# Fourier transform and gated feed-forward layer on one core: moving setup work off VectorE, one gather ahead of a bulk load, half-width copies, and a new order of the last output pieces

## The chip, the core and the metric

The kernel runs on one core of a Trainium2 chip. The metric is device time in microseconds (us) of that core; the time before is 616.64 us, the median of three runs (616.6 to 617.27). The span in a trace is some 1.9 us shorter than the time of the same run, so I compare times with times and spans with spans.

## The reference

```python
def _attn_ref(x):                       # x: (8, 3008, 256), float32
    X = np.fft.fft(x, axis=1)           # along the sequence
    X = np.fft.fft(X, axis=2)           # along the width
    return X.real.astype(np.float32)

def _moe_ref(x, w_gate, w_val, w_out):  # x: (24064, 256); 256 -> 1536 -> 256
    g = x @ w_gate
    gelu = 0.5 * g * (1.0 + erf(g * inv_sqrt2))
    val = x @ w_val
    return (gelu * val @ w_out).astype(np.float32)
# reference: _moe_ref(_attn_ref(x).reshape(24064, 256), ...)
```

## The kernel before

The sequence transform of 3008 points is done as two transforms of 32 and 94 points. x is folded first (row i plus its mirror image), so x is read twice: forward rows by a plain DMA and mirrored rows by an indirect gather. For the first batch both go through GpSimd's queue with a cast to bf16, in this order:

```python
def opening():
    ...                                  # stage[0]: forward rows 9-16 and 0, by another queue
    pool_consts()
    index_consts(0)
    cast_mirror(0, 9, 8)                 # gather, rows 9..16
    pool_consts2()
    cast_mirror(0, 5, 4)                 # gather, rows 5..8
    cast_forward(0, 1, 8)                # plain, rows 1..8
    index_consts(1)
    cast_mirror(0, 0, 1)                 # gather, row 0
    cast_mirror(0, 1, 4)                 # gather, rows 1..4
    ...                                  # weights, then x of the second batch, same queue
```

VectorE folds the rows into `eo_sb`. TensorE transforms them (`s1`), ScalarE copies the result to `A_sb`; column transforms (`ch`) give four pieces of `Z_sb`, and `tp_e` gives E and O, the two halves of the transformed x that the gate and value products read. `warm(n)` multiplies zeros n times to keep TensorE's clock up. The opening of the program is one straight list of such calls:

```python
    fold_piece(9, 4)
    first, second = fold_ops(0, 13, 4, nc.vector)
    first(); t_reduced(); second()
    s1(0, 2, 0)(); s1(0, 2, 1)()
    t_sin(); gelu_table(); warm(6)
    fold_piece(5, 4)
    s1(0, 1, 0)(); s1(0, 1, 1)()
    fold_piece(0, 1)
    fold_piece(1, 4)
    ...
```

The last chunk of tokens is written in eight pieces, (sub, half) from (3,0) to (2,1). Each is a product of twelve matmuls into a PSUM buffer (PSUM is the memory that TensorE writes), a copy to an SBUF buffer, and a store. There are three such SBUF buffers, and a buffer is free only when its store has landed:

```python
def osb_tile():
    return work([128, 2, C], FP32, "osb", 3, "out_sb")

            if last(ci):
                osb = osb_tile()
                if sign == 0:
                    nc.vector.tensor_copy(osb[:m, 0, :], pso[:m, half])
                    store(b, ci, sub, 0, osb[:, 0, :], nc.sync)
                else:
                    nc.scalar.activation(osb[:m, 1, :], pso[:m, half], AF.Copy)
                    store(b, ci, sub, 1, osb[:, 1, :], nc.scalar)
```

Of the kernel before, what the change touches and what calls it, by code (L numbers as in the profile page):

```python
# [9 lines left out]
FP32 = mybir.dt.float32  # L10
BF16 = mybir.dt.bfloat16
AF = mybir.ActivationFunctionType
# [16 lines left out]
def kernel(  # L29
# [225 lines left out]
    rd = work([128, 2 * NGP + NK], FP32, "Z", 1, "rd")  # L255
    cf, cr, cd = (work([128, C], FP32, t, 4, f"small_{i}") for i, t in enumerate(("v", "v", "v")))
    tf, tr, td = (work([128, 128], FP32, t, 3, f"small_t{i}") for i, t in enumerate(("ve", "ve", "ve")))
    w_raw = work([128, 2, 2, F], BF16, "h", 2, "w_raw")
# [69 lines left out]
    def g_phases():  # L328
# [14 lines left out]
        c = _sub(rd, [[1, NGP]], 0, part_num=NP)  # L343
        nc.vector.scalar_tensor_tensor(c, d1, -1.0, d1, op0=ALU.mult, op1=ALU.max)
        nc.vector.tensor_scalar(c, c, -0.25, None, op0=ALU.add)
        nc.vector.scalar_tensor_tensor(d0, r[:, 0:NK], MAGIC, f[:, 0:NK], op0=ALU.subtract, op1=ALU.subtract)

# [40 lines left out]
    def identities():  # L388

        nc.vector.tensor_scalar(  # L390
            _sub(II, [[128, 3], [1, 128]], 0), _sub(row_c, [[0, 3], [1, 128]], 0), col_p, None, op0=ALU.is_equal)
        nc.vector.tensor_scalar(II[:, 1, 1, :], row_c, col_p, -1.0, op0=ALU.is_equal, op1=ALU.mult)

# [196 lines left out]

    def tp_e(b, gi, g=0, engine="A", tag=None):
        def run():
            st = state(b)
            if b not in EO_bufs:
                EO_bufs[b] = EO_tiles()
            ps = psum(tag) if tag else ps_any(b)
            for pair, o, n in pairs(gi):
                nc.tensor.matmul(  # L598
                    ps[:, o : o + n], st["Z"][:, pair, g * 128 : g * 128 + 128], _sub(TP, [[1, n]], g * 128),
                    start=True, stop=True)  # L600
            if b == 0 and g == 1:
                for pair, o, n in pairs(gi):
                    nc.tensor.matmul(  # L603
                        ps[0:1, o : o + n], st["Z"][:, pair, 128:129], _sub(TP, [[1, n]], 0), start=True, stop=True)
            n = chunk_len[gi]
            dst = _sub(EO_bufs[b][g], [[1, n]], chunk_off[gi])
            if engine == "A":
                nc.scalar.activation(dst, ps[:, :n], AF.Copy)  # L608
            else:
                nc.vector.tensor_copy(dst, ps[:, :n])  # L610
        return run
# [65 lines left out]
    def ffn_work(b):  # L677
# [126 lines left out]
        for ci in range(NG):  # L804
            nsub = (chunk_len[ci] + 127) // 128
            parts = {k: [f(ci, fc) for fc in range(NFC)] for k, f in (
                ("G", l1_gate), ("V", l1_value), ("g", l1_gate2), ("v", l1_value2))}
            subs = [nsub - 1, *range(nsub - 1)] if last(ci) else range(nsub)
            l2s = [l2_piece(ci, s, g, f) for s in subs for g in range(2) for f in range(0, NFC, L2P)]
            chunks.append((parts, l2s))  # L810
# [3 lines left out]
    def opening():  # L814
# [10 lines left out]
        cast_mirror(0, 5, 4)  # L825
        cast_forward(0, 1, 8)
        index_consts(1)
        cast_mirror(0, 0, 1)
        cast_mirror(0, 1, 4)
        for f0, n in ((0, 256), (256, 256), (512, 512), (1024, 512)):  # L830
# [23 lines left out]
        vec_fills()  # L854
        warm(16)
        cw_phases()
        g_phases()
        columns = t_columns()
        g_rows(9, 7)
        cw_reduced()  # L860
        vec_fills2()
        vec_consts2()
        identities()
        cw_magnitude()
        cw_sin()
        cw_rest()
        g_ends()
        g_rows(1, 8)
        t_phases(columns)
        fold_piece(9, 4)  # L870
        first, second = fold_ops(0, 13, 4, nc.vector)
        first()
        t_reduced()
        second()
        s1(0, 2, 0)()
        s1(0, 2, 1)()
        t_sin()
        gelu_table()
        warm(6)
        fold_piece(5, 4)  # L880
        s1(0, 1, 0)()
        s1(0, 1, 1)()
        fold_piece(0, 1)
        fold_piece(1, 4)
        s1(0, 3, 0)()
        s1(0, 3, 1, "V")()
        warm(1)
        s1(0, 0, 0)()
        s1(0, 0, 1, "V")()
        minus, copies = [], []  # L890
        make_w(0, 0, 256, m_at=minus, tag="o", copy_at=copies)()
        t_write()
        for pp in range(2):
            ch(0, pp, qs=(0,))()
            ch(0, pp, "V", qs=(1,))()
        copies.pop()()
        make_w(1, 0, 256, m_at=minus, m_engine="V", tag="v", copy_at=copies)()
        tp_e(0, 0, 0, "A", tag="v")()
        tp_e(0, 0, 1, "V", tag="dft")()
        copies.pop()()  # L900
        minus[0]()
# [4 lines left out]
    def plan():  # L906
# [10 lines left out]
        for s, f in (  # L917
                (0, make_w(0, 256, 256, m_engine="P")), (0, make_w(1, 256, 256, engine="V", m_engine="P")),
                (1, make_w(1, 512, 512, (1,), m_engine="P")), (1, lambda: load_wo(0)), (1, lambda: load_wo(1)),
                (2, make_w(0, 512, 512, (0,), "V")), (2, make_w(0, 512, 512, (1,))),  # L920
                (3, make_w(1, 512, 512, (0,))), (4, make_w(1, 1024, 512, (1,), "V")),
# [146 lines left out]
```

## Time and profile before

| what | before |
|---|---|
| span of the profiled run, us | 614.93 |
| TensorE busy | 605.4 us, 98% |
| first fold starts / last fold ends | 8.26 / 13.41 |
| last of ScalarE's and VectorE's copies to `A_sb` ends | 14.89 |
| last of the four copies to `Z_sb` ends | 16.35 |
| O complete | 17.91 |
| first gelu starts | 18.37 |
| last output copy starts | 610.95 |

From the first gelu on TensorE is full, so the table is read from the top: each row is a point that the next one waits for.

Three lines of the timeline of the kernel before (start, length, engine, line, operation, tiles, count) are the issue of the forward rows 1 to 8, the tiny column products that prepare the last transform, and the first fold of rows 5 to 8.

```profile
4.85 0.60 POOL L185 DMA_DIRECT2D xb<-in_x_dram  x1
...
7.57 1.27 PE L397 MATMUL ps_v<-one,par 1*128 1x1 f32 x10
...
11.35 0.19 DVE L221 TENSOR_TENSOR eo_sb<-xb 94x8 bf16<-94x8 bf16 x1
```

The transfer's landing records (16 rings, one for each DMA engine) run from 10.21 to 11.16 us, and VectorE folds the rows at 11.35.

At the end, in the same view, the last product and the last copy:

```profile
609.44 1.47 PE L778 MATMUL ps_g<-Wo_sb,h_sb 128*128 128x256 bf16 x12
...
610.95 0.38 ACT L794 ACTIVATE out_sb<-ps_g 128x256 f32<-128x256 f32 x1 [2.24 <-DMA out_dram<-out_sb]
```

The product ends at 609.44 + 1.47 = 610.91, and the copy starts 0.04 us later. So the copy waits for TensorE, although the bracket puts its 2.24 us of idle time down to a store, the releaser that came last by the profile's account.

### The profile page before, as it was taken

What the parts mean: (1) busy time and instruction counts of PE and PEld (TensorE: products, weight loads), DVE (VectorE), ACT (ScalarE), POOL (GpSimd) and SP (SyncE); (2) the same over time, 40 slices, a digit from 0 to 9 for tenths busy, and PEclk for the clock granted to TensorE, in tenths of its full rate; (3) what the DMA queues carried; (4) which work ended last, traced back from release to release, by engine and by line L of the source; (5) the groups of instructions that cost most, each with busy time, mean ns of one, the idle gap of its engine ahead of it and who ended that gap; (6) DMA issues with size and microseconds to landing.
All of it is one profiled execution on the core that took longest, in us unless ns stands there. A gap on an engine that the chain in (4) does not pass through costs nothing.

```text
span 614.9 us, 12747 instructions
## 1 busy us (share of the span) xinstructions
PE 605.4 (98%) x4181; PEld 406.9 (66%) x4229; DVE 577.3 (94%) x941; ACT 425.0 (69%) x824; POOL 508.9 (83%) x513
## 2 busy tenths in 40 slices
PE   8999999999999999999999999999999999999997
PEld 4466666666666666666666666666666666666666
DVE  8799999999999999999999999999999999999992
ACT  6888677777776777667766677666776676666661
POOL 8999899999987999789997899869997655565551
PEclk8999999999999999999999999999999999999999
DMA  9962834547253364532553344533213223111123
GB/s 175 200 137 57 237 95 117 141 116 189 80 144 92 100 163 119 140 100 58 157 150 94 106 107 107 146 102 100 64 49 77 62 87 78 42 46 47 37 51 83
DMA packets 52466, 65.40 MB, mean 106 GB/s; under 512 B 7629, under 2 KB 47278, under 8 KB 50004
## 3 DMA queue, kind: packets, MB, share of 16 engines
q1 hardware_dynamic: 45472, 49.03, 30.5%
q0 software_dynamic: 6608, 15.29, 11.7%
q8 instruction: 33, 0.54, 0.4%
q10 hardware_dynamic: 320, 0.26, 0.2%
q14 instruction: 33, 0.27, 0.2%
HBM read 39.65 MB, written 30.17 MB: 114 GB/s over the span
## 4 chain that ended last, share of the span: by engine, by line
PE 94%; DVE 2%; issue 1%; DMA 1%; ACT 1%; SPq 1%; POOL 0%; DVEq 0%; POOLq 0%; ACTq 0%
PE ps_o L778 39%; PE ps_g L681 29%; PE ps_v L681 20%; PE ps_dft L562 2%; PE ps_dft L598 2%; DMA out_dram<-out_sb 1%; PE ps_dft L451 1%; SPq L675 1%; PE ps_o L847 0%; PE ps_dft L542 0%; ACT gelu_sb L705 0%; ACT gelu_sb L714 0%; DVE v_sb L751 0%; POOL h_sb L753 0%; PE ps_dft L603 0%
## 5 line engine op out<-in xcount | busy, mean ns | idle before, releaser
L753 POOL TENSOR_TENSOR h_sb<-gelu_sb,v_sb 128x512 bf16<-128x512 bf16 (+1 forms) x280 | 319.9, 1147 | 87.0 <-DVE v_sb L751 79.0
L778 PE MATMUL ps_o<-Wo_sb,h_sb 128*128 128x256 bf16 (+1 forms) x2232 | 334.3, 272 | 0.0
L778 PEld LDWEIGHTS <-h_sb 128*128 128x128 bf16 (+1 forms) x2304 | 228.6, 100 | 111.2 <-POOL h_sb L753 1.0
L733 DVE SCALAR_TENSOR_TENSOR ve_sb<-EB_sb,yw,ps_v 128x512 f32<-128x512 bf16 (+1 forms) x280 | 206.3, 737 | 18.6 <-PE ps_v L681 16.6
L705 ACT ACTIVATE gelu_sb<-ps_g 128x512 bf16<-128x512 f32 (+1 forms) x288 | 169.3, 588 | 78.1 <-PE ps_g L681 62.9
L749 DVE TENSOR_TENSOR h_sb<-gelu_sb,ps_v 128x512 bf16<-128x512 bf16 (+1 forms) x280 | 190.0, 678 | 0.7
L681 PEld LDWEIGHTS <-W_sb 128*128 128x128 bf16 x1440 | 138.4, 98 | 78.0 <-issue 1.7
L751 DVE SCALAR_TENSOR_TENSOR v_sb<-ve_sb,ps_v 128x512 f32<-128x512 f32 (+1 forms) x280 | 187.4, 669 | 0.0
L714 ACT ACTIVATE gelu_sb<-ps_g 128x512 bf16<-128x512 f32 (+1 forms) x288 | 168.6, 585 | 0.0
L681 PE MATMUL ps_g<-O_sb,W_sb 128*128 128x512 bf16 (+1 forms) x530 | 159.1, 374 | 2.7 <-DVE O_sb L610 0.3
L681 PE MATMUL ps_g<-E_sb,W_sb 128*128 128x512 bf16 (+1 forms) x287 | 107.6, 375 | 0.7 <-ACT gelu_sb L714 0.5
L681 PE MATMUL ps_v<-O_sb,W_sb 128*128 128x512 bf16 (+1 forms) x288 | 108.0, 375 | 0.0
L681 PE MATMUL ps_v<-E_sb,W_sb 128*128 128x512 bf16 (+1 forms) x288 | 107.9, 375 | 0.0
L798 ACT ACTIVATE out_sb<-ps_o 128x512 f32<-128x512 f32 x92 | 55.0, 598 | 34.2 <-PE ps_o L778 34.1
L229 POOL TENSOR_TENSOR eo_sb<-ab_sb 94x512 bf16<-94x512 f32 (+1 forms) x70 | 77.7, 1112 | 0.4
L565 ACT ACTIVATE S_sb<-ps_dft 96x512 bf16<-96x512 f32 x56 | 33.2, 592 | 29.7 <-PE ps_dft L562 29.7
L222 POOL TENSOR_TENSOR ab_sb<-x_raw,x_raw 94x508 f32<-94x508 f32 (+1 forms) x30 | 33.0, 1101 | 0.0
L225 POOL TENSOR_TENSOR ab_sb<-x_raw,x_raw 94x508 f32<-94x508 f32 (+1 forms) x30 | 33.0, 1100 | 0.0
L562 PE MATMUL ps_dft<-eo_sb,G 94*96 94x256 bf16 x119 | 22.3, 272 | 0.0
L608 ACT ACTIVATE E_sb<-ps_dft 128x512 bf16<-128x512 f32 (+1 forms) x23 | 13.6, 590 | 12.0 <-PE ps_dft L598 12.0
L608 ACT ACTIVATE O_sb<-ps_dft 128x512 bf16<-128x512 f32 (+1 forms) x22 | 13.0, 590 | 11.6 <-PE ps_dft L598 11.1
L163 POOL DMA_INDIRECT x_raw<-in_x_dram,idx x18 | 17.2, 957 | 2.9 <-issue 0.8
(151 smaller groups left out, 207.6 us busy)
## 6 DMA issues: line engine op xcount, KB each, us to landing
out_dram<-out_sb SPq DMA_DIRECT2D x364, 64.0 KB
x_raw<-in_x_dram SPq DMA_DIRECT2D x10, 768.0 KB
Z_sb<-z SPq DMA_DIRECT2D x7, 768.0 KB
z<-S_sb SPq DMA_DIRECT2D x7, 576.0 KB
EB_sb<-yrow SPq DMA_DIRECT2D x6, 376.2 KB
z<-S_sb SPq DMA_DIRECT2D x7, 192.0 KB
x_raw<-in_x_dram SPq DMA_DIRECT2D x2, 640.0 KB
x_stage<-in_x_dram SPq DMA_DIRECT2D x1, 768.0 KB
```

The costliest lines, as they stand in the source:

```text
L229: eng.tensor_tensor(_sub(eo, [[C, nj], [1, 128]], j0 * C + g * 128), ab(0, 0, [[1, 128]]), ab(1, 0, [[1, 128]]), op=op)
L562: nc.tensor.matmul(ps[:96, q * C : (q + 1) * C], G[:, j, :], _sub(eo, [[1, C]], j * C), start=(j == js[0]), stop=(j == js[-1]))
L565: nc.scalar.activation(_sub(st["S"], [[1, 512]], (4 * jg + 2 * half) * C, part_num=96), ps[:96, :], AF.Copy)
L681: nc.tensor.matmul(ps[:, :n], W[nm, part][:, fs], src, start=start, stop=stop, **kw)
L705: nc.scalar.activation(gl[:, 0, :n], pg[:, :n], AF.Gelu)
L714: nc.scalar.activation(_sub(gl, [[-1, n]], TOK + n - 1), pg[:, :n], AF.Gelu)
L733: nc.vector.scalar_tensor_tensor(ve[:, :n], EB_bufs[b][:, c0 : c0 + n], yw[:, fc : fc + 1], pv[:, :n], op0=ALU.mult, op1=ALU.add)
L749: nc.vector.tensor_tensor(st["h"][:, fc, 0, :n], gl[:, 0, :n], pv[:, :n], op=ALU.mult)
L751: nc.vector.scalar_tensor_tensor(_sub(vv, [[-1, n]], n - 1), ve[:, :n], 2.0, pv[:, :n], op0=ALU.mult, op1=ALU.subtract)
L753: nc.gpsimd.tensor_tensor(st["h"][:, fc, 1, :n], gl[:, 1, :n], vv[:, :n], op=ALU.mult)
L778: nc.tensor.matmul(pso[:m, half], st["h"][:, fc, sign, h0 : h0 + m], Wo_sb[:, fc, :], start=(fc == 0 and not (first and sign)), stop=(fc = ...
L798: nc.scalar.activation(_sub(osb, [[1, 2 * C]], 0, part_num=m), pso[:m, :], AF.Copy)
```

## The change

Its intent is to start the first full product sooner, and to take two late waits of TensorE away. The prediction numbers six parts: 1, setup from VectorE to ScalarE, and the phases of the last transform ahead of x; 2, the gather and the fold of row 0 ahead of rows 5 to 8; 3, fewer fillers; 4, column copies in halves; 5, a copy from ScalarE to VectorE; 6, the order of the last pieces. The diff, cut to its core:

```diff
-        nc.vector.scalar_tensor_tensor(c, d1, -1.0, d1, op0=ALU.mult, op1=ALU.max)
+        nc.scalar.activation(c, d1, AF.Abs)
+        cw_reduced()
 ...
-        nc.vector.tensor_scalar(
-            _sub(II, [[128, 3], [1, 128]], 0), _sub(row_c, [[0, 3], [1, 128]], 0), col_p, None, op0=ALU.is_equal)
-        nc.vector.tensor_scalar(II[:, 1, 1, :], row_c, col_p, -1.0, op0=ALU.is_equal, op1=ALU.mult)
+        nc.scalar.activation(apart[:, 0:128], row_c, AF.Abs, scale=-1.0, bias=col_p)
+        nc.scalar.activation(
+            _sub(II, [[128, 3], [1, 128]], 0), _sub(apart, [[0, 3], [1, 128]], 0), AF.Relu, scale=-1.0, bias=1.0)
+        nc.scalar.activation(II[:, 1, 1, :], II[:, 0, 0, :], AF.Copy, scale=-1.0)
 ...
-    def tp_e(b, gi, g=0, engine="A", tag=None):
+    def tp_e(b, gi, g=0, engine="A", tag=None, part=slice(0, 4)):
 ...                                        (products and copy of pairs(gi)[part] only)
-            subs = [nsub - 1, *range(nsub - 1)] if last(ci) else range(nsub)
-            l2s = [l2_piece(ci, s, g, f) for s in subs for g in range(2) for f in range(0, NFC, L2P)]
+            order = [(s, g) for s in range(nsub) for g in range(2)]
+            if last(ci):
+                order = [(nsub - 1, 0), (0, 0), (nsub - 1, 1), *order[1:-2]]
+            l2s = [l2_piece(ci, s, g, f) for s, g in order for f in range(0, NFC, L2P)]
 ...
         cast_mirror(0, 5, 4)
-        cast_forward(0, 1, 8)
         index_consts(1)
         cast_mirror(0, 0, 1)
+        cast_forward(0, 1, 8)
         cast_mirror(0, 1, 4)
 ...
-        warm(16)
+        warm(8)
         cw_phases()
+        identities()
         g_phases()
         columns = t_columns()
-        g_rows(9, 7)
-        cw_reduced()
+        warm(8)
 ...
+        t_phases(columns)
+        t_reduced()
+        g_rows(9, 7)
 ...
-        warm(6)
+        warm(3)
+        fold_piece(0, 1)
+        s1(0, 3, 0)()
+        s1(0, 3, 1)()
+        warm(2)
         fold_piece(5, 4)
         s1(0, 1, 0)()
         s1(0, 1, 1)()
-        fold_piece(0, 1)
         fold_piece(1, 4)
-        s1(0, 3, 0)()
-        s1(0, 3, 1, "V")()
-        warm(1)
 ...
+        copies[0]()
 ...
-        tp_e(0, 0, 0, "A", tag="v")()
-        tp_e(0, 0, 1, "V", tag="dft")()
-        copies.pop()()
+        for g in range(2):
+            tp_e(0, 0, g, "A", tag="v", part=slice(0, 2))()
+            tp_e(0, 0, g, "V", tag="dft", part=slice(2, 4))()
+        copies[1]()
 ...
-                (2, make_w(0, 512, 512, (0,), "V")), (2, make_w(0, 512, 512, (1,))),
+                (2, make_w(0, 512, 512, (0,), "V")), (2, make_w(0, 512, 512, (1,), m_engine="V")),
```

More of the change, by code (lines that the diff above doesn't have):

```diff
@@ L256 @@
     cf, cr, cd = (work([128, C], FP32, t, 4, f"small_{i}") for i, t in enumerate(("v", "v", "v")))
+    apart = work([128, C], FP32, "v", 4, "apart")
     tf, tr, td = (work([128, 128], FP32, t, 3, f"small_t{i}") for i, t in enumerate(("ve", "ve", "ve")))
@@ L343, in g_phases @@
         c = _sub(rd, [[1, NGP]], 0, part_num=NP)
-        nc.vector.scalar_tensor_tensor(c, d1, -1.0, d1, op0=ALU.mult, op1=ALU.max)
+        nc.scalar.activation(c, d1, AF.Abs)
+        cw_reduced()
+        nc.vector.scalar_tensor_tensor(d0, r[:, 0:NK], MAGIC, f[:, 0:NK], op0=ALU.subtract, op1=ALU.subtract)
         nc.vector.tensor_scalar(c, c, -0.25, None, op0=ALU.add)
-        nc.vector.scalar_tensor_tensor(d0, r[:, 0:NK], MAGIC, f[:, 0:NK], op0=ALU.subtract, op1=ALU.subtract)
     def g_rows(j0, nj):
@@ L596, in run @@
             ps = psum(tag) if tag else ps_any(b)
-            for pair, o, n in pairs(gi):
+            for pair, o, n in pairs(gi)[part]:
                 nc.tensor.matmul(
@@ L601, in run @@
             if b == 0 and g == 1:
-                for pair, o, n in pairs(gi):
+                for pair, o, n in pairs(gi)[part]:
                     nc.tensor.matmul(
                         ps[0:1, o : o + n], st["Z"][:, pair, 128:129], _sub(TP, [[1, n]], 0), start=True, stop=True)
-            n = chunk_len[gi]
-            dst = _sub(EO_bufs[b][g], [[1, n]], chunk_off[gi])
+            o, n = pairs(gi)[part][0][1], sum(w for _, _, w in pairs(gi)[part])
+            dst = _sub(EO_bufs[b][g], [[1, n]], chunk_off[gi] + o)
             if engine == "A":
-                nc.scalar.activation(dst, ps[:, :n], AF.Copy)
+                nc.scalar.activation(dst, ps[:, o : o + n], AF.Copy)
             else:
-                nc.vector.tensor_copy(dst, ps[:, :n])
+                nc.vector.tensor_copy(dst, ps[:, o : o + n])
         return run
@@ L854, in opening @@
         vec_fills()
-        warm(16)
+        warm(8)
         cw_phases()
+        identities()
         g_phases()
         columns = t_columns()
-        g_rows(9, 7)
-        cw_reduced()
+        warm(8)
         vec_fills2()
         vec_consts2()
-        identities()
         cw_magnitude()
@@ L866, in opening @@
         cw_rest()
+        t_phases(columns)
+        t_reduced()
+        g_rows(9, 7)
         g_ends()
         g_rows(1, 8)
-        t_phases(columns)
+        t_sin()
         fold_piece(9, 4)
-        first, second = fold_ops(0, 13, 4, nc.vector)
-        first()
-        t_reduced()
-        second()
+        fold_piece(13, 4)
         s1(0, 2, 0)()
         s1(0, 2, 1)()
-        t_sin()
         gelu_table()
-        warm(6)
+        warm(3)
[3 more added lines that the diff above has]
+        warm(2)
         fold_piece(5, 4)
@@ L895, in opening @@
             ch(0, pp, "V", qs=(1,))()
-        copies.pop()()
         make_w(1, 0, 256, m_at=minus, m_engine="V", tag="v", copy_at=copies)()
-        tp_e(0, 0, 0, "A", tag="v")()
-        tp_e(0, 0, 1, "V", tag="dft")()
-        copies.pop()()
+        for g in range(2):
+            tp_e(0, 0, g, "A", tag="v", part=slice(0, 2))()
+            tp_e(0, 0, g, "V", tag="dft", part=slice(2, 4))()
+        copies[1]()
         minus[0]()
```

## The prediction

> **What bounds the kernel now.** I read the page first: TensorE is busy nearly always.
>
> ```profile
> PE 605.4 (98%) x4181; PEld 406.9 (66%) x4229; DVE 577.3 (94%) x941; ACT 425.0 (69%) x824; POOL 508.9 (83%) x513
> ```
>
> So only TensorE's gaps, and stretches in which it is busy but slow, are to be had. The list of TensorE's waits over the whole span holds all its gaps:
>
> ```profile
> PE ps_o L847 <- DVE col L316: 1.2, 1, 1.2
> PE ps_g L681 <- ACT gelu_sb L714: 0.5, 1, 0.5
> PE ps_dft L778 <- POOL h_sb L753: 0.3, 1, 0.3
> PE ps_g L681 <- DVE O_sb L610: 0.3, 1, 0.3
> PE ps_v L520 <- DVE eo_sb L225: 0.3, 1, 0.3
> PE ps_g L520 <- issue: 0.2, 1, 0.2
> ```
>
> They add to 2.8 us. All but two lie in the first 18 us; the 0.5 lies at 25.1 us and the 0.3 of L778 at 602.4 us. Between them TensorE never waits. But "busy" contains filler: L847 multiplies zeros to keep the clock up. The chain of waits shows the opening, in order of time (start, length, what):
>
> ```profile
> 9.03 0.61 DVE eo_sb L225
> ...
> 10.03 2.14 PE ps_o L847 x6
> 12.17 0.32 PE ps_dft L520 x4
> ...
> 13.61 0.34 PE ps_o L847
> 13.96 0.17 PE ps_g L520 x4
> ...
> 16.86 0.33 PE ps_dft L603 x4
> 17.19 0.02 issue
> 17.21 0.70 DVE O_sb L610
> 17.92 0.04 issue
> 17.96 0.38 PE ps_g L681
> ```
>
> Read: folded x (eo_sb) goes through the first transform (L520), the second (L542, L598, L603), is copied to E and O, and the first full gate product stands at 17.96. From there TensorE is full. Two things there are not arithmetic: the filler before 12.17, and the 0.70 copy of O, during which TensorE has nothing. The table of stretches (length, PE busy and count, granted clock, DMA share, GB/s) says why filler took 0.36 apiece:
>
> ```profile
> 6.90:10.30 3.40, 2.90 (x24) 1.00 1.05 192
> 10.33:13.74 3.41, 3.41 (x24) 0.50 1.21 167
> ```
>
> The clock was halved for 3.41 us after a stretch that held much idle or tiny work.
>
> **What the Trainium skill says.** "TensorE: Matmul & The Clock Gate", section "What's actually happening", gives a free-running activity window of 3413 ns whose business sets the clock to half or full. The trace agrees: half clock from 10.33 to 13.74 us; and the first filler, 0.43 us apart until 6.9 us against some 0.22 afterwards, shows a cold start that the clock column, which has no record there, does not. "ScalarE: Activation LUTs", section "What ACT_TABLE_LOAD costs", gives an ACTIVATE as 186 ns plus 0.833 ns an element, and about 93 ns more for each pointer operand. The trace agrees: 0.29 us for 128 elements, 0.40 with a pointer, 0.59 for 512. The same page's "Rules for kernel authors" sends relu and the like to VectorE as the faster engine; here VectorE's fp32 128x384 identity costs 0.60 us, and the formula gives ScalarE 0.60 too with a pointer, so what counts is who is on the path. "DMA: Bandwidth & Descriptors", section "Two DMAs through the same engine are not ordered", says descriptors of one queue start in order. The landing records agree: the five transfers of x by GpSimd's queue are complete at 8.00, 8.69, 11.16, 11.43 and 12.38 us, in the order of issue, and that queue is never empty from 5.1 to 33.5 us.
>
> **Part 1, VectorE's preparation.** Two identity instructions (0.60 and 0.28 us) and |d| (0.58) leave VectorE, 1.46 us; the reduction of the last transform's phases (0.23 + 0.29) comes ahead of the first fold. On ScalarE come, as estimates by the formula: 0.39 (|i-j|, pointer), 0.60 (relu over 384), 0.29 (sign), 0.53 (Abs of 408). Placed by their waits: Abs begins when d1 is ready at 4.79 and the identities are out, about 4.9, so it ends near 5.45; VectorE has its small work meanwhile. The twiddle sines then end near 6.5, the phases near 7.35, VectorE's reduction near 7.95, G's first rows near 8.25. All are ready when x is: its last gather lands at 8.00. The first fold began at 8.26, so this part wins at most 0.15 there. The next fold wins 0.5 more, its interleaved reduction being gone (11.44 to about 10.8), but the one after it awaits a transfer anyway.
>
> **Part 2, the gather of row 0 first.** In the queue it moves ahead of the forward rows 1 to 8. I estimate its transfer at 0.27 us (11.43 - 11.16), so row 0 is there near 9.0 instead of 11.43, the forward rows near 11.43 instead of 11.16, the last gather at 12.38 as before. The forward issue slips from 4.85 to about 6.85 us, as the index constants and one 1 us gather come ahead. An empty queue later shows 1.8 to 2.0 us from issue to the first packet, so packets would be ready at about 8.65, just as rows 5 to 8 of the mirror end (8.69): no hole, barely. VectorE then folds row 0 before the long wait, rows 5 to 8 from 11.5 to 12.35, rows 1 to 4 from 12.45 to 13.3. Before, the last fold ended at 13.41: 0.1 us.
>
> **Part 3, filler and order on TensorE.** Of 23 fillers 21 remain; after row 0 only rows 5 to 8 and 1 to 4 remain in L520, so TensorE no longer drags 0.8 us of row 0's group and a 0.34 filler behind the last folds. Products for rows 1 to 4 end near 13.55 instead of 14.30. But their copies are the next bound: ScalarE's table load starts near 10.95 (was 11.26), and its five A copies then follow 0.37 apart; the last ends near 14.3 (was 14.65). The column transform L542 can start at 14.35, not 14.73. This part is worth 0.35 to 0.4, not the 0.75 that TensorE alone shows.
>
> **Part 4, copies in halves.** W's copy moves ahead of the Z copies, into ScalarE's idle time (0.62 us before the first Z copy). E and O are copied as 256-wide halves: 0.39 on ScalarE (as the Z copies there), 0.43 on VectorE, both engines at once. Before: last Z copy ends 16.36, O ends 17.90. After: halves of E at 16.6, of O near 17.2, when the Z copies end at 16.0. The Z part is the 0.4 already counted; the halves add 0.3 to 0.45, but the gelu is held by ScalarE's W copy and minus copy (both behind the halves), so I count 0.35. The first gate product of O moves from 17.96 to near 17.2: 0.75 us in all for parts 1 to 4.
>
> **Part 5, not in the headline.** The minus copy of 512 gate columns goes from ScalarE to VectorE. In the chain:
>
> ```profile
> 23.38 0.60 ACT W_sb L459
> 23.98 0.58 ACT W_sb L475
> 24.56 0.49 ACT gelu_sb L705
> 25.05 0.50 ACT gelu_sb L714
> 25.54 0.04 issue
> ```
>
> TensorE waits 0.51 for that last gelu to free its PSUM buffer. Without L475 the two gelus end 0.5 earlier; VectorE has 0.82 us idle before 25.08 for a 0.75 us instruction. I count 0.5.
>
> **Part 6, the end.** The final output pieces are reordered so that a piece that needs only VectorE's product comes before the one that needs GpSimd's last:
>
> ```profile
> 602.74 0.31 PE L778 MATMUL ps_dft<-Wo_sb,h_sb 128*97 128x256 bf16 x1 [0.30 <-POOL h_sb L753]
> ```
>
> TensorE then has 1.3 us of work in place of this 0.30 wait. After it pieces follow without a gap, so the end moves by 0.3.
>
> **Sum.** 0.75 + 0.5 + 0.3 = 1.55 us; 616.64 - 1.55 = 615.1.
>
> **Rivals.** (a) The clock. With less filler and more waiting, the window before 13.74 may be judged idle, and the half clock then falls on 13.74 to 17.15, where L451, L542 and L598 are on the path. Before, the window from 6.90 with 2.90 us busy was judged idle though only some 0.5 us was a gap, since tiny products fill it; the change puts the same tiny L397 products among the first fillers. I estimate 1.1 to 1.3 us lost on the path (some twelve products of 256 columns at 0.21 instead of 0.11, and the waits between). The result would be near 616.2. For it: the window is independent of the kernel's start, so it can hit any run. Against it: the last folds' products are spread up to 13.6. I give it one in three. (b) The transfer wait takes over: if GpSimd's later issue leaves a hole of 0.5 us in the queue, the last fold ends after 13.41 and parts 2 and 3 come to nothing; the weights behind are later too. The value weights for L451 at 20.55 land at 19.48, so an opening faster by over 1.0 us would wait there anyway. Result 615.6 to 615.9. (c) GpSimd: its fold of rows 1 to 4 of the second batch ends at 53.95 and TensorE uses it at 54.36. GpSimd begins that work after weights and x that the queue brings, not earlier than before, but has 0.54 and 0.69 us of idle time at 42 to 45 us to make up. So TensorE can gain some 1.6 us before it meets this: a cap just above my 1.25 up to that point.
>
> **Range and chances.** All parts whole, with a lucky clock: 0.75 may become 1.1, so 614.6, less some 0.3 for repeats (the three before spread by 0.67). The clock rival with a hole in the queue: 616.3. Range 614.3 to 616.3. Two per cent is 12.3 us; nothing here is of that size, either way: faster 0.005, same 0.99, slower 0.005.
>
> **What would show it.** Right: the first O-product of L681 starts near 17.2; no wait of L681 for the gelu at 25 us; no wait of L778 for GpSimd at the end; E and O written in 0.39 to 0.43 us pieces by two engines; the first fold still starts after 8.0. Wrong: half clock between 13.7 and 17.2; the fold of rows 5 to 8 starting after 11.8; a new wait of TensorE on GpSimd's eo_sb near 53 us, or on the value weights near 19.8; VectorE at 25 us late with h because of the minus copy.

## The result, and the profile after

The changed kernel took 617.96 us in the median of four runs (616.09 to 618.52), against 616.72 for the kernel before (616.6 to 617.27). The ratio is 1.0013, with a 95% interval of 0.9991 to 1.0035. It is "the same" by the 2% rule, but the predicted gain of 1.55 us did not come. The later runs put the change on the slow side by about a microsecond.

The top of the page shows a TensorE that is busier, not freer:

```profile
PE 608.1 (99%) x4227; PEld 406.8 (66%) x4227; DVE 575.8 (93%) x939; ACT 426.8 (69%) x829; POOL 508.7 (83%) x513
```

The list of TensorE's waits (line, what it waited for, total us, times, longest) is short:

```profile
PE ps_v L523 <- DVE eo_sb L222: 1.4, 1, 1.4
PE ps_o L853 <- DVE col L317: 1.2, 1, 1.2
```

The two waits that parts 5 and 6 aimed at are gone: none for the gelu at 25 us, none for GpSimd at 602 us. The wait for O before the first gate product is gone as well. In their place stands one wait of 1.4 us, of the first transform for a fold, in the opening. The timeline after shows what that fold waited for:

```profile
4.75 2.29 PE L400 MATMUL ps_v<-one,par 1*128 1x1 f32 x10
...
6.56 0.61 POOL L185 DMA_DIRECT2D xb<-in_x_dram  x1
...
8.15 0.35 DVE L266 TENSOR_SCALAR small_t<-small_t 128x128 f32<-128x128 f32 x1 [1.03 <-ACT small_t L407]
...
13.08 0.19 DVE L221 TENSOR_TENSOR eo_sb<-xb 94x8 bf16<-94x8 bf16 x1 [1.23 <-DMA xb<-in_x_dram]
```

Read them against the lines of before. The forward rows are issued at 6.56 instead of 4.85, and the fold of rows 5 to 8 starts at 13.08 instead of 11.35, after 1.23 us in which VectorE had nothing else. The column products take 2.29 us instead of 1.27, because they now stand in TensorE's cold start; the reduction that depends on them makes VectorE wait 1.03 us, and the first fold starts at 8.74, not 8.26. The chain of waits names the same transfer (start, length, what):

```profile
6.56 6.43 DMA xb<-in_x_dram
12.99 0.03 issue
...
18.53 0.91 PE ps_g L684 x3
```

6.56 + 6.43 = 12.99. The landing records explain the figure: thirteen of the 16 rings are complete by 11.30, as I had estimated, and three come at 12.53, 12.76 and 12.99. A fold needs all partitions, so it needs the last ring. The first packet of these rows moves at 8.38, 1.82 us after the issue; of their 96 packets of 4 KB, 83 had started by 10.70, and the other thirteen started between 10.95 and 12.36.

The stretches after (length, PE busy and count, PEld, VectorE, ScalarE and GpSimd likewise, granted clock, DMA share, GB/s), one window of the clock each:

```profile
10.27:13.68 3.41, 2.24 (x24) 1.19 (x22) 1.92 (x7) 3.39 (x8) 3.02 (x5) 1.00 1.13 159
13.68:17.10 3.42, 2.90 (x30) 2.07 (x31) 2.76 (x10) 2.63 (x7) 2.87 (x5) 1.00 1.31 193
```

This run had the full clock from 10.27 us on, where its clock records begin. Ahead of that its fillers stand 0.43 us apart, as in a cold start, where those of before do so only until 6.9: with the column products between the fillers the cold start can last longer (it ended by 4.54 in e1, e3 and e6, which have the same order). What this trace lost after 10.27 is not the clock's.

At 25 us, the counterpart of the chain that the prediction shows for part 5:

```profile
25.28 0.74 DVE L480 TENSOR_SCALAR W_sb<-ps_dft,keep 128x512 bf16<-128x512 f32 x1
...
26.11 0.38 PE L684 MATMUL ps_g<-E_sb,W_sb 128*128 128x512 bf16 x1
```

VectorE makes the minus copy in 0.74 us, and L684 follows with no wait. And the end, the counterpart of the two lines of before:

```profile
609.60 1.47 PE L781 MATMUL ps_g<-Wo_sb,h_sb 128*128 128x256 bf16 x12
...
611.77 0.38 ACT L797 ACTIVATE out_sb<-ps_g 128x256 f32<-128x256 f32 x1 [0.89 <-DMA out_dram<-out_sb]
```

The last product ends at 609.60 + 1.47 = 611.07, but its copy starts at 611.77. This time the store in the bracket is the true cause: the copy waits 0.70 us for a free buffer.

The ledger of the two traces, after minus before, reads the same instructions in both:

| point | after minus before, us |
|---|---|
| last fold ends (15.05 against 13.41) | +1.64 |
| last copy to `Z_sb` ends (17.51 against 16.35) | +1.16 |
| first gelu (19.48 against 18.37) | +1.11 |
| past the place at 25 us | +0.53 |
| at 600 us | +0.66 |
| last product of the end (611.07 against 610.91) | +0.16 |
| last copy starts (611.77 against 610.95) | +0.82 |
| span (616.08 against 614.93) | +1.15 |

So the opening lost 1.11, the minus copy won 0.58, the new order won 0.50 on TensorE and lost 0.66 at the copies, and the last store added 0.33 (the span ends 4.31 us after the last copy starts, before 3.98).

### The profile page after: what moved, and what is told of

It reads as the page before. It is cut to its first block, busy times and chain, and to the rows that moved or that the text cites. A ratio compares the mean times of both kernels' runs of the same rounds, so it can differ in the third digit from the quotient of the medians. Undisturbed runs are those within 1.5% of the kernel's fastest.

```text
span 616.1 us, 12787 instructions
## 1 busy us (share of the span) xinstructions
PE 608.1 (99%) x4227; PEld 406.8 (66%) x4227; DVE 575.8 (93%) x939; ACT 426.8 (69%) x829; POOL 508.7 (83%) x513
## 4 chain that ended last, share of the span: by engine, by line
PE 95%; DMA 2%; POOL 1%; DVE 0%; issue 0%; SPq 0%; ACT 0%; DVEq 0%; POOLq 0%; ACTq 0%
PE ps_o L781 40%; PE ps_g L684 30%; PE ps_v L684 20%; PE ps_dft L565 2%; PE ps_dft L601 2%; DMA xb<-in_x_dram 1%; DMA out_dram<-out_sb 1%; PE ps_dft L454 1%; POOL xb L163 0%; PE ps_dft L545 0%; SPq L678 0%; PE ps_v L781 0%; DVE out_sb L794 0%; PE ps_dft L606 0%; DVE eo_sb L222 0%
## 5 line engine op out<-in xcount | busy, mean ns | idle before, releaser
L684 PEld LDWEIGHTS <-W_sb 128*128 128x128 bf16 x1440 | 138.2, 98 | 77.5 <-issue 1.0
L684 PE MATMUL ps_g<-O_sb,W_sb 128*128 128x512 bf16 (+1 forms) x576 | 169.0, 375 | 0.0
L684 PE MATMUL ps_v<-O_sb,W_sb 128*128 128x512 bf16 (+1 forms) x288 | 108.0, 375 | 0.0
L684 PE MATMUL ps_v<-E_sb,W_sb 128*128 128x512 bf16 (+1 forms) x288 | 108.0, 375 | 0.0
L684 PE MATMUL ps_g<-E_sb,W_sb 128*128 128x512 bf16 (+1 forms) x288 | 107.9, 375 | 0.1
L163 POOL DMA_INDIRECT x_raw<-in_x_dram,idx x18 | 17.2, 957 | 2.9 <-DVE v_sb L754 0.8
```

What stands on the lines that cost most here:

```text
L684: nc.tensor.matmul(ps[:, :n], W[nm, part][:, fs], src, start=start, stop=stop, **kw)
```

## The experiments

Twelve kernels ran, in three groups of four, each group on a chip of its own and beside the kernel before. All gave correct results. Three questions were open. Why did three rings of one transfer come late: because the transfer was issued late, or because a gather now stood directly ahead of it? Why did the last copies wait: the three buffers, or something that came from the opening? And how much of the time is the clock, which half of the runs may show and the profiled run did not?

Milestones of the traces, in us. "Rows 1–8" is the issue of the forward transfer and its last ring; the "half clock" column gives the stretch of half clock in that run's records before 20 us (which begin between 4 and 10 us, so the cold start ahead of them isn't in it).

| kernel | rows 1–8: issue, last ring | last fold ends | last `Z_sb` copy ends | first gelu | last output copy | half clock |
|---|---|---|---|---|---|---|
| before | 4.85, 11.16 | 13.41 | 16.35 | 18.37 | 610.95 | 10.33–13.74 |
| after | 6.56, 12.99 | 15.05 | 17.51 | 19.48 | 611.77 | none |
| e1 after again | 6.55, 12.88 | 14.93 | 18.33 | 20.30 | 612.27 | 10.72–17.55 |
| e2 old tail | 6.55, 12.48 | 14.59 | 17.04 | 19.01 | 611.06 | none |
| e3 old queue order | 4.84, 11.93 | 14.28 | 18.53 | 20.53 | 612.13 | 11.36–18.19 |
| e4 part 5 alone | 4.84, 11.22 | 14.18 | 16.74 | 18.76 | 610.73 | 10.69–14.10 |
| e5 issue later | 6.17, 11.03 | 13.78 | 18.01 | 20.05 | 612.58 | 10.83–17.65 |
| e9 issue later still | 6.55, 13.21 | 15.44 | 17.90 | 19.92 | 612.58 | 10.10–13.52 |
| e6 gather earlier | 5.56, 10.98 | 13.99 | 17.57 | 19.83 | 611.68 | 10.95–17.77 |
| e7 part 6 alone | 4.84, 10.82 | 13.42 | 16.36 | 18.38 | 610.62 | 9.91–13.32 |
| e8 best | 4.85, 11.01 | 13.42 | 16.24 | 18.26 | 609.70 | 9.31–12.72 |
| e10 more filler | 6.55, 13.38 | 15.44 | 17.99 | 19.96 | 611.60 | 12.33–15.74 |
| e11 best with halves | 4.85, 11.26 | 13.49 | 15.95 | 17.92 | 609.52 | none |
| e12 mended | 5.56, 10.45 | 13.54 | 16.55 | 18.52 | 610.11 | none |

### e1: the changed kernel again, no edit

> The changed kernel unaltered, for its spread and a second trace. In its first trace the forward rows 1 to 8 of x were complete only at 12.99 us (three of the sixteen DMA rings 1.2 to 1.7 us behind the others), VectorE waited 1.23 us for them, TensorE 1.40. Theory T (the new order in GpSimd's queue makes that transfer late): the wait of TensorE on the fold of rows 5 to 8 is there again, within 1.0 to 1.6 us, and the time is 617.5 to 618.3. Rival C (chance: slow packets fell on that transfer once): the wait is under 0.4 us in this trace and the time nearer 616.5. In both, the last copy of the output waits some 0.9 us for a store to free its buffer.

Measured: 618.24 us (617.13 to 618.67, six runs), before on the same chip 616.82 (616.35 to 618.76, eleven runs), ratio 1.0014 [1.0, 1.0027]. The three late rings are there again, at 12.81 to 12.88. This profiled run caught the half clock too; two windows (columns as above):

```profile
10.72:14.13 3.41, 1.83 (x13) 0.93 (x13) 1.38 (x8) 2.42 (x5) 2.92 (x5) 0.50 1.08 153
14.13:17.55 3.42, 3.42 (x27) 2.54 (x25) 2.07 (x8) 2.13 (x5) 2.80 (x5) 0.50 1.29 195
```

The last fold ends even a little sooner than in the first trace (14.93 against 15.05), yet the `Z_sb` copies end 0.82 later. From the last fold to the last of those copies it is 3.40 us here and 2.46 at full clock. The clock's share of the times can be counted, since a half-clock window of 3.41 us lowers the mean clock of a run by 0.5 × 3.41 / 616 = 0.28%, and two of them to 0.994 or less. Of ten runs of the changed kernel (the first four and these six), five had a mean clock of 0.994 or less and took 618.45 us on average; the other five took 617.27. The difference of 1.18 us is about what two half windows cost. Of the 29 runs of the kernel before on the three chips, three were at 0.994 or less (618.84), and the other 26 averaged 616.84. So the change makes the double window much more frequent, and without it the kernel still loses 617.27 − 616.84 = 0.43 us; that is not clear of noise, as those five runs lie between 616.09 and 618.06.

### e2: the changed kernel with the old order at the end

```diff
-                order = [(nsub - 1, 0), (0, 0), (nsub - 1, 1), *order[1:-2]]
+                order = [*order[-2:], *order[:-2]]
```

> The changed kernel with the old order of the last output pieces. Theory S (the new order makes the last copies wait for stores to free the three output buffers; it costs 0.5 us of the end instead of winning 0.3): 0.4 to 0.7 us faster than the changed kernel of the same rounds, the last copy following TensorE's last product at once, and the 0.3 us wait of TensorE on GpSimd's last product back. Rival (the new order wins 0.3 as predicted, and what is lost at the end of the first trace is the transfer noise of that run): 0.3 slower than the changed kernel.

Measured: 617.5 us (616.87 to 619.32, six runs), ratio 1.0016 [0.9999, 1.0032]. The time decides nothing: its scatter is wider than the effect. The trace does. The last product ends at 609.55 + 1.47 = 611.02, and the last copy starts at 611.06, directly behind it; the 0.30 wait of TensorE for GpSimd at the end is back. The old order costs TensorE 0.3 and keeps the last copy free of stores; of those before it, one still starts 0.63 us after its product.

### e3: the changed kernel with the old order of GpSimd's queue

```diff
         cast_mirror(0, 5, 4)
+        cast_forward(0, 1, 8)
         index_consts(1)
         cast_mirror(0, 0, 1)
-        cast_forward(0, 1, 8)
         cast_mirror(0, 1, 4)
```

> The changed kernel with the old order in GpSimd's queue only: forward rows 1 to 8 are issued ahead of the index constants and the gather of row 0. The fold order stays, so VectorE must wait for row 0 at about 11.4 us and folds rows 5 to 8 from about 11.9, rows 1 to 4 until about 13.6. Theory T: the forward transfer is complete near 11.2 again, with no ring far behind, and the time is 0.4 to 0.8 us below the changed kernel's. Rival C (chance): the same time as the changed kernel within 0.3, or 0.3 slower, since row 0 comes later.

Measured: 616.67 us (616.46 to 617.89, six runs), ratio 0.9994 [0.9982, 1.0006], against 1.0014 for the changed kernel in the same rounds. The queue order alone is thus worth about 0.2% of 616, some 1.2 us, though the two intervals overlap, and about half of it may be the clock: without the runs at a mean clock of 0.994 or less the means are 616.58 (four runs) and 617.17 (two, of e1). In its trace the first fold starts at 7.97 and the forward rows are complete at 11.93. The last fold still ends at 14.28, not 13.41, because VectorE now stands 1.61 us before row 0, whose gather lands after the forward rows again (at 12.20) while its fold comes first. So here too the folds wait for a transfer, only another one, and issue order and fold order belong together.

### e4: the kernel before with part 5 alone

```diff
-                (2, make_w(0, 512, 512, (0,), "V")), (2, make_w(0, 512, 512, (1,))),
+                (2, make_w(0, 512, 512, (0,), "V")), (2, make_w(0, 512, 512, (1,), m_engine="V")),
```

> The kernel before with the minus copy of 512 gate columns on VectorE as its only edit. My count: TensorE's 0.51 us wait for the gelu at 25 us is gone and the time is 0.4 to 0.55 us below the kernel before. Rival (a later wait of TensorE on ScalarE or GpSimd takes it back by 40 us): same within 0.15 us.

Measured: 616.0 us (615.64 to 616.56, five runs), ratio 0.9981 [0.9968, 0.9994]. The wait of L681 for the gelu is gone from TensorE's list. This single argument is better than the whole change. Its opening is that of before, yet in its trace the last fold ends at 14.18 instead of 13.41: the gather of rows 1 to 4 was complete only at 13.32 (before 12.38), 1.56 us after its median ring. So a ring can fall far behind in an opening that nobody changed.

### e5 and e9: the kernel before, with the forward rows issued later and no gather ahead of them

Both put harmless work of GpSimd ahead of the issue; e5 clears 768 columns, e9 1200.

```diff
         cast_mirror(0, 5, 4)
-        cast_forward(0, 1, 8)
+        nc.gpsimd.memset(W_sb[:, 4, 0:1200], 0.0)   # e5: 0:768
         index_consts(1)
+        cast_forward(0, 1, 8)
         cast_mirror(0, 0, 1)
         cast_mirror(0, 1, 4)
```

> The kernel before, in which GpSimd issues the forward rows 1 to 8 later: a filling memset (of a weight area that is overwritten afterwards) and the index constants come first, so that the issue falls near 6.4 us instead of 4.85; the gather of row 0 stays behind it. Theory L (the transfer is late on some rings because it is issued under 2 us before the queue reaches it): three to five rings complete at 12.2 us or later, VectorE waits for it about 1 us more, and the time is 0.5 to 1.1 us above the kernel before. Rival G (it is the gather of row 0 directly ahead of it in the queue that holds rings up): all rings complete by about 11.5, and the time is the kernel before's within 0.3 us.

Measured for e5: 617.14 us (616.71 to 618.36, four runs), before 616.74 (616.27 to 617.06, seven runs), ratio 1.0004 [0.9988, 1.0021]. The issue came at 6.17, and all rings were complete by 11.03: no late ring. (Its `Z_sb` copies are late in the table because this run had half clock from 10.83 to 17.65.) That spoke against a late issue as the cause, until I saw that it was still 0.4 us earlier than in the changed kernel. So e9 went on to the same 6.55.

> As e5, with a longer filling memset: the forward rows 1 to 8 are issued near 6.6 us, as late as in the changed kernel (6.56), with the gather of row 0 behind them. In e5 (issue 6.17) all rings were complete by 11.03 and theory L seemed to fall; its lead was 2.1 us, though, and an idle queue takes 1.8 to 2.0 us from issue to first packet. Theory L with that threshold: some rings complete at 11.9 us or later here. Theory LG (a late issue hurts only with the row 0 gather directly ahead): all rings complete by 11.5, as in e5.

Measured for e9: 618.6 us (618.11 to 619.66, four runs), before 616.97 (616.32 to 618.91, eleven runs), ratio 1.0029 [1.0011, 1.0046]. This is the slowest kernel. Its timeline:

```profile
6.55 0.57 POOL L185 DMA_DIRECT2D xb<-in_x_dram  x1
...
13.30 0.19 DVE L221 TENSOR_TENSOR eo_sb<-xb 94x8 bf16<-94x8 bf16 x1 [1.12 <-DMA xb<-in_x_dram]
```

Fifteen rings were complete by 11.46 and one came at 13.21, with the gather still behind. The late ring came back with the issue time alone. Over all traces the split of this transfer is clean: with the issue at 6.55 to 6.56 (after, e1, e2, e9, e10) the last ring came between 12.48 and 13.38; with the issue at 6.17 or before (the other nine) it came by 11.93 at the latest.

What it is about the later issue stays open. I had thought of the lead: in before the first packet of these rows moves 3.06 us after the issue, in the changed kernel 1.82. But in e5 it is 1.85, and no ring is late; in e6 (below) it is 1.64, and one ring is 0.6 us late, not 1.7. So the packets begin on time everywhere, and yet with the latest issue some rings fall behind. Only one ring did so in e9, where three to five did with the gather ahead, so the gather may add to it. One trace of a kind doesn't tell. The packets show how a ring falls behind: single ones stall. The median 4 KB packet of these rows takes 0.32 us in every trace. The longest of the 96 took 0.94 to 2.14 us in the five traces with the latest issue, 1.31 in e6 and 1.57 in e3, whose last rings came 1.0 and 1.1 us after the median one, and 0.44 to 0.72 in the other seven. What stalls a packet no trace here tells.

### e6: the changed kernel with row 0's gather still ahead, both moved forward in the queue

```diff
-        cast_mirror(0, 5, 4)
         index_consts(1)
         cast_mirror(0, 0, 1)
         cast_forward(0, 1, 8)
+        cast_mirror(0, 5, 4)
         cast_mirror(0, 1, 4)
```

> The changed kernel with the gather of row 0 and the forward rows 1 to 8 issued before the gather of rows 5 to 8 of the mirror: the gather of row 0 is still directly ahead of the forward rows, but the forward issue falls near 5.5 us and the queue reaches it near 7.8. Theory L: the rings complete together again, all of x rows 1 to 8 and mirror 5 to 8 by about 11.5 us, VectorE's wait falls from 1.2 to under 0.4 us, and the time is 0.6 to 1.1 us below the changed kernel's 618.1, near 617.2. Rival G: rings late by 1.2 to 1.8 us as before, time near 618. (If the lead is still too short, rings late under L too: then e5 alone tells.)

Measured: 617.01 us (616.3 to 618.04, four runs), ratio 1.0001 [0.9984, 1.0017]. The forward rows, issued at 5.56 directly behind the gather of row 0, had fifteen rings by 10.35 and the last at 10.98. The gather ahead does no harm by itself. What is late now is the gather of rows 5 to 8, which slipped behind; its last ring is complete at 11.93:

```profile
12.03 0.19 DVE L221 TENSOR_TENSOR eo_sb<-xb 94x8 bf16<-94x8 bf16 x1 [1.01 <-DMA xb<-in_x_dram,idx]
```

The same wait of VectorE, 1.01 us, for another transfer: the last fold ends at 13.99.

### e7: the kernel before with the new order at the end alone

The edit is part 6 of the diff above, in the kernel before.

> The kernel before with the new order of the last output pieces as its only edit. Theory S (three output buffers are too few for that order): TensorE's 0.3 us wait for GpSimd is gone, yet the last copy waits 0.5 to 0.9 us for a store, and the time is 0.3 to 0.6 us above the kernel before. Rival: 0.3 us below it, as I predicted.

Measured: 616.71 us (615.84 to 617.46, four runs), ratio 1.0 [0.9984, 1.0017]. In its trace TensorE's wait is gone, and the span is 614.61, or 0.32 shorter. The store theory had expected a loss here, and it missed:

```profile
610.62 0.38 ACT L794 ACTIVATE out_sb<-ps_g 128x256 f32<-128x256 f32 x1 [1.22 <-PE ps_g L778]
```

The last copy starts 0.04 us after the product's end (609.11 + 1.47 = 610.58). An earlier one had waited for a store (the copy of (1,1), which ended its 2.90 us of idle time at 609.02, 1.06 after its product's end), but the delay ran out before the last. With three buffers copies wait for stores in either order, but longer in the new one: 0.70 to 2.04 us at the longest in a trace, with the old order 0.37 to 0.68. The last copy waits in some runs only: 0.70 us in the first trace, 0.46 in e1, 0.35 in e6, not in e3, e7 and e10. The time cannot tell a gain of 0.3 us from none.

### e8: the kernel before with part 5, part 6, and twice the output buffers

The three buffers that the last pieces share become six, by taking every other one from a tag that is idle by then.

```diff
+        turn_out = [0]
 ...
-                    osb = osb_tile()
+                    turn_out[0] += 1
+                    osb = osb_tile() if turn_out[0] % 2 else work([128, 2, C], FP32, "ve", 3, "out_ve")
 ...                                        (and the edits of e4 and e7)
```

> The kernel before with the minus copy on VectorE, the new order of the last pieces, and six output buffers at the end (every other piece in buffers of VectorE's that are free by then). Theory S: no copy at the end waits for a store by more than 0.1 us, the last copy comes 0.3 us earlier, and with the 0.5 us of the minus copy the time is 0.8 to 1.0 us below the kernel before. Rival (the stores themselves, not the buffers, bound the end): 0.4 to 0.55 below, the minus copy alone.

Measured: 615.29 us (615.2 to 615.59, four runs), ratio 0.9976 [0.9959, 0.9993]. It beats both kernels, and it is the fastest by the trace but for e11.

```profile
608.19 1.47 PE L779 MATMUL ps_g<-Wo_sb,h_sb 128*128 128x256 bf16 x12
...
609.70 0.38 ACT L796 ACTIVATE out_ve<-ps_g 128x256 f32<-128x256 f32 x1 [2.24 <-DMA out_dram<-out_ve]
```

The last copy follows its product (609.66) directly. Against before the last product ends 1.25 us sooner: 0.11 were there at the first gelu, some 0.5 are the minus copy, 0.50 the new order as in the ledger (0.30 of it the wait for GpSimd), and about 0.14 I cannot name.

### e10: the changed kernel with more filler

```diff
-        warm(2)
+        warm(5)
         fold_piece(5, 4)
```

> The changed kernel with five filling products instead of two ahead of the fold of rows 5 to 8, where TensorE waits 1.25 to 1.4 us anyway. Theory K (in about half of the changed kernel's runs the window before 14 us counts as idle, TensorE runs at half clock from about 10.7 to 17.6, and such a run is 1.3 us longer): no run has a mean clock of 0.994 or less, all are near 617.2, the median 0.5 to 0.9 below the changed kernel's 618.1. Rival (the half clock comes from the window before, and filler there changes nothing, or filler delays the next product): runs of both sorts as before, median 617.9 to 618.3.

Measured: 617.39 us (617.03 to 620.2, six runs), ratio 1.0012 [0.9994, 1.0031]. None of the six runs had a mean clock of 0.994 or less, where five of ten of the changed kernel had; that is suggestive for so few runs, not proof. One run took 620.2 with a mean clock no lower than 0.997, which I cannot explain. The profiled run still had one half-clock window, 12.33 to 15.74. The transfer came late as in the changed kernel (last ring 13.38), so filler at best removes the clock's part and leaves the late rings.

### e11: e8 with the copies in halves (part 4)

The edit is part 4 of the diff above, in e8.

> The fastest kernel so far (e8: minus copy on VectorE, new order of the end with six buffers; 615.3) plus the column copies in halves with W's copy ahead of the Z copies. My prediction's count for the halves: 0.35 us, so 614.9. Rival (TensorE's products for E and O take longer in four groups than in two, as the changed kernel's trace has it: 1.49 us from the last Z copy to O, against 1.54): within 0.15 us of e8, 615.15 to 615.45.

Measured: 615.73 us (615.38 to 616.09, five runs), ratio 0.9979 [0.9966, 0.9992]. Its ratio equals that of e8 (0.9976, from another chip) within the intervals. In the traces O is complete 1.48 us after the last `Z_sb` copy, against 1.56 in e8 and in before: the halves are worth 0.08 us.

### e12: the changed kernel mended

The queue of e6, the six buffers of e8, and the filler of e10 in the changed kernel.

> The changed kernel with its three faults mended: queue order of e6, six output buffers at the end, five filling products. If transfers, buffers and clock are the whole of its loss: 615.2 to 616.0, 0.8 to 1.5 us below the kernel before, with no copy waiting for a store at the end and a wait of TensorE on the fold of rows 5 to 8 under 0.6 us. If something else in the opening holds it back: above 616.3.

Measured: 616.41 us (615.91 to 617.46, five runs), ratio 0.9994 [0.998, 1.0008]. The forward rows are complete at 10.45 and the last fold ends at 13.54; no copy at the end waits for a store, and the last starts at 610.11. But the opening wins nothing over before, since a new wait of TensorE has come up, for ScalarE's copies of the first transform:

```profile
15.04 0.39 PE L545 MATMUL ps_dft<-II,A_sb 128*128 128x256 bf16 x2 [0.67 <-ACT A_sb L529]
```

ScalarE's table load ended late here, and the five copies stand one behind the other from 13.04 to 14.99. The column products were cold in this run too (2.29 us), so the phases and the load came late: the load started at 11.64, as in the first trace, and at 10.91 or 10.92 where the column products were warm (e1, e3, e6). Mended, the change is as good as before by the intervals, and slower on average than e11 on the same chip, which leaves the first folds alone (615.38 to 616.09, against 615.91 to 617.46).

## Why the prediction was wrong, step by step

**Part 2 failed, and it is the main term of the miss.** The step was: "packets would be ready at about 8.65, just as rows 5 to 8 of the mirror end (8.69): no hole, barely", and from it "rows 5 to 8 from 11.5 to 12.35". The first half held: the first packet moved at 8.38, and the queue had no hole. That is partly luck, for both figures behind it were read too sharply: the 8.69 rests on 4 of 16 landing records (traces with all 16 have 8.89 in e7 to 9.43 in e4), and of the sixteen later issues on an empty queue in that trace seven took 2.5 to 3.8 us to the first packet, not 1.8 to 2.0. What failed is what I concluded from it, "the forward rows near 11.43": I took a queue that starts on time for a transfer that ends on time. Thirteen rings were complete by 11.30; three came up to 1.7 us later. The fold of rows 5 to 8 started at 13.08, and the last fold ended at 15.05 instead of the 13.3 of my working: 1.75 us. That covers nearly the whole miss of the opening. My first O-product was to start at 17.2 and started at 19.05, 1.85 late. The forward rows are not the only late transfer: the gather of rows 1 to 4 behind them was complete at 13.95 instead of the 12.38 of my working, and VectorE came to its rows at 14.22, so forward rows in time would by themselves have moved the last fold by little. That it comes with the late issue, e9 shows with one trace and one late ring, and e5 and e6 that the gather or a little delay alone do not bring it; why packets of some rings stall and not of all, stays open.

**Part 1 was mis-sized, but hidden.** "The first fold still starts after 8.0" came true, yet at 8.74 instead of some 8.1. I had the phases near 7.35, without doubling the column products at TensorE's cold start: 2.29 us, where a warm run of the same kernel had them in 1.24 (e1, 4.40 to 5.64) and started its first fold at 8.08. Since VectorE then waited for the transfer anyway, it cost nothing in the changed kernel. It shows in e12, where the transfer is on time. ScalarE's new instructions cost what "ScalarE: Activation LUTs", section "What ACT_TABLE_LOAD costs", gives: 0.52 us for the relu of 384 elements, by its formula without a pointer 0.51 (I had counted one with a pointer), and 0.39 for 128 with a pointer.

**Part 3 is not shown.** From the last fold to the last `Z_sb` copy it took 2.94 us before and 2.46 after at full clock, 0.48 less, where I had counted 0.35 to 0.4. But the first of these is a trace that had half clock until 13.74, and with full clock there the old fillers and order take 2.46 too: in e9 from 15.44 to 17.90, in e11 (part 4, not part 3) from 13.49 to 15.95. So the clock explains the difference as well. One step failed: the table load was to start near 10.95, and it did so at 11.64, since the column products were cold.

**Part 4 was mis-sized.** I counted 0.35 for the halves; the runs show 0.08 (1.56 to 1.48 us from Z to O in both pairs). Each copy became shorter, O's last one 0.42 us instead of 0.69. But the products that feed them became four groups in place of two, from 17.32 to 18.53, 1.2 us instead of 1.0 (16.16 to 17.17 before), with VectorE idle 0.31 us between. I had let the products come for nothing.

**Part 5 was right.** I counted 0.5; the ledger shows 0.58 in the changed kernel, and e4 alone is faster by 0.19% of 616, about 1.2 us in times, within an interval of 0.4 to 2.0. Its chain loses the ScalarE copy exactly as the working has it.

**Part 6 was right on TensorE and wrong at the end.** "After it pieces follow without a gap, so the end moves by 0.3" held for the products (0.50 in the ledger). The step that failed is the word "end": I followed TensorE and not the buffers behind it. The order (3,0), (0,0), (3,1) brings the copies closer together at the start, three buffers are taken, and a buffer is free only when its store has landed. The last copy came 0.70 us after its product, and the end came another 0.33 later after it: SyncE issued the last store 0.59 us after that copy's end (612.74), before 0.03. In e7 the delay ran out before the last piece, and six buffers (e8, e12) take it away.

**The rivals.** (a), the clock, I gave one in three. By their mean clocks it came in five of ten runs, at 1.18 us, as estimated (1.1 to 1.3), though in e1's trace with two windows of half clock and not the one that I had counted. It is not what made the profiled run slow. (b) named the right transfer, but as a hole of 0.5 us in the queue that only cancels parts 2 and 3: "Result 615.6 to 615.9". The queue had no hole, and the stray rings pushed the folds 1.64 us past their old place. (c), GpSimd's later fold as a cap, was not met, since nothing came early.

**The sum again.** In the trace: +1.11 in the opening instead of −0.75, −0.58 at 25 us instead of −0.5, +0.13 of drift that I cannot name, and +0.49 at the end instead of −0.3. It makes +1.15, where I had −1.55. The clock adds half of 1.18 in the mean. My range ended at 616.3 with both bad rivals at once, but my own figures for them add to more: 615.6 to 615.9 with the hole, and 1.1 to 1.3 for the clock, make 616.7 to 617.2. At its lower end 616.64 − 1.1 − 0.5 − 0.3 is 614.7, not 614.6.

## What to carry to other kernels

A transfer that moves back in its queue is judged by the landing of its last ring, not by its first packet: here the packets began on time, and VectorE still waited 1.23 us for three rings of sixteen, so keep what the path needs issued early and measure where it goes wrong (here between 6.17 and 6.55 us, as far as one trace of most kernels tells). When pieces at the end are reordered, count the buffers until their stores land, for TensorE's gain is lost there. And try the small independent edits alone first: an engine argument, an order and three buffers (e8, 615.29 us) beat the whole rearrangement.

## What the Trainium skill lacked or had wrong

- "DMA: Bandwidth & Descriptors", section "Latency and other measured facts", gives about 1 µs to the first byte for GpSimd's DMAs and does not say from which point it counts. Of the sixteen gathers that GpSimd issues on an empty queue from 60 us on in the trace of before, nine took 1.66 to 2.01 us from the start of the issue to the first packet, or 0.70 to 0.97 from its end; the other seven took 2.53 to 3.79 from the start.
- No page ties it to the time of the issue that rings of one transfer fall far behind with its first packets on time. The same section of "DMA: Bandwidth & Descriptors" has two engines, 7 and 15, as usually slower than the others; which engine a late ring belongs to, the traces here do not tell. With the issue at 6.55 to 6.56 us, one to five of 16 rings came more than 0.7 us after the median one, the last 1.5 to 2.4 us after it. With an earlier issue the last came 0.4 to 1.1 us after it (nine traces).
- "TensorE: Matmul & The Clock Gate", section "What's actually happening", ties the clock to idle and busy windows but does not say how busy is busy. A window with 2.90 us busy of 3.41, more than a third of it ten 1-column products, was followed by half clock (6.90 to 10.30 before); the same stretch in e11, 2.96 us busy from 7.01 to 10.42, was not. One with 2.24 us of filler and 96-column products was not (10.27 to 13.68 after), and one with 1.83 us was (e1).
